# Polysketch attention and a mixture of experts on one core: attention in fewer, wider units at fixed half steps, and fewer changes of TensorE's tile

## The chip, the core and the metric

The kernel runs on 1 core of one Trainium2 chip. The metric is device microseconds (us) of one execution. The kernel is one launch; everything below is inside it.

## What is computed

The reference, cut to what matters (B = 4 batches, H = 4 heads, S = 1088 tokens, head width 32; 4352 tokens of width 128; E = 4 experts with 1024 hidden columns):

```python
def phi(x):
    a = np.einsum('rd,bhsd->bhsr', S1, x)      # r = 8
    b = np.einsum('rd,bhsd->bhsr', S2, x)
    return np.einsum('bhsi,bhsj->bhsij', a, b).reshape(*x.shape[:-1], r * r)
q_p, k_p = (phi(q), phi(k))
kv = np.einsum('bhsf,bhsd->bhfd', k_p, v)
z = np.sum(k_p, axis=2)
attn = np.einsum('bhsf,bhfd->bhsd', q_p, kv) / (np.einsum('bhsf,bhf->bhs', q_p, z)[..., None] + 1e-06)
...
x = attn.transpose(0, 2, 1, 3).reshape(B * S, H * D)
p = domain_probs / (domain_probs.sum(-1, keepdims=True) + 1e-09)
for e in range(E):
    h = np.maximum(x @ w1[e], 0.0)
    out += p[:, e:e + 1] * (h @ w2[e])
```

## The kernel before, in words

**Experts.** Token columns are worked in chunks (`CHUNKS`): 128, 448, 512, seven of 448, and 128 columns, eleven in all. A chunk has 16 steps (4 experts by 4 pairs of 128-wide blocks of hidden columns), a step two half steps, one for each block. The counter `now` numbers the half steps through the whole kernel: chunk m begins at 32m. In chunks 1 to 9 a block's first layer is three fp32r matmuls over 128x128 tiles: xa by wa (L1174), xb by wb (L1175), then ACT scales the partial sum in place in PSUM (L1176, in `first`), and the third, xd by wd (L1226, in `third`), is added behind it. ACT takes relu into ha (L1230), DVE makes hb (L1202) and for two blocks at once hd (L1205, in `lower`). The second layer's passes over ha, hb and hd, or one plain fp32 pass for some blocks, are L1295 in `passed`; `DEAL` sets how many half steps behind its block each pass is issued, `due` holds them and `behind` issues them. Experts 0 and 1 of chunk 1 have a plain fp32 second layer (L1276). POOL weights a result by its gate (L1334, L1336). The gates are loaded by SP (L385), which waits until POOL has left the tile. `turn_back` turns and stores a chunk's output.

**First and last chunk.** With 128 columns they are plain fp32. Their matmuls go through `both` and `on_side` (L257 to L267): a product is done as pairs of matmuls on half tiles, 128 rows by 64 columns of TensorE, the two halves by turns. In the profile all half-tile matmuls have the line L261 and the tile 128*64; an fp32 matmul on half tiles leaves two records.

**Keys.** For each batch `key_pieces` has the pieces: turns of the keys on DVE (L412), projections with full tiles (L456), sums, products on DVE, then `key_sums` (36 half-tile matmuls of 66 columns, `vx` by `kp`) and `key_blocks` (the tile kvx).

**Queries.** The tokens of a batch are cut into units (`UNITS`): [128, 448, 512], [448, 448, 192], [256, 448, 384], [512, 320, 256]. The first two units of batch 0 are worked at the start; the ten others are `later`. A later unit passes through these parts: `unit_turn` (DVE, L596); `unit_project` (four half-tile matmuls with sx, an ACT copy to qs at L787, SP's writes of it to the DRAM tile qd at L789 and its loads back from there, each row repeated, into qp at L796 and qb at L798 or L801); `unit_product`, twice (DVE, L810); `unit_visit` (half-tile matmuls of 66 columns, kvx by qp); `attend_inverse` (DVE, L699 and L704); `attend_scale` (L712); and `unit_out` (turn on DVE at L725, SP's writes to the DRAM tile xd at L744, and loads from there into `ring` or x_last at L753). A chunk's columns are read out of `ring` by ACT (xa, L925) and DVE (xb and xd, L928) in `token_parts`, four steps before the chunk begins. Together on PE come, as one piece named "visit": the key sums of the next batch where the unit is a batch's last, the projection of the next unit, and the products of this one.

**What sets the order.** The instructions of each engine stand in program order. `lay_plan` makes a list of pieces, each with a cost in us and, for some, a piece that it must follow by a number of half steps (`LAND` is 6 for a product behind its visit). In each half step `work` adds to a credit by `rate` and `room` (L1371 to L1386 and L1461 to L1484) and issues pieces from the list's head while the credit lasts; `until_there` issues what is missing when a chunk is near. `holds` counts PSUM banks that attention holds; while there are any, the credit is at least 0.01. PSUM has 6 banks in the pool `ps_h` (first layer and attention) and 2 in `ps_o`. SP issues nearly all DMAs, in program order: the writes and loads above, gates and outputs.

Of the kernel before, what the change touches and what calls it, by code (L numbers as in the profile page):

```python
# [24 lines left out]
def kernel(  # L25
# [26 lines left out]
    P = 128  # L52
# [10 lines left out]
    QW = 512  # L63
    CW = 512
    GE = 160
    LA = 2
    LAND, EARLY = 6, 14
# [15 lines left out]
    UNITS = [[P, 448, 512], [448, 448, 192], [256, 448, 384], [512, 320, 256]]  # L83
# [7 lines left out]
    W2_AT = (36, 38), (41, 43), (45, 47), (65, 67)  # L91
    TOKENS_AT = 11, 12

    CHUNKS = [P, 448, 512] + [448] * 7 + [P]
# [424 lines left out]
    holds = [0]  # L519

    def held(x):
        holds[0] += 1
        return x

    def free(n=1):
        holds[0] = max(0, holds[0] - n)

    def key_pieces(b):

        for r in range(3):  # L530
            add(0.69 if r < 2 else 0.23, lambda r=r: key_turn(b, r), f"turn{r}")
        values, kf = value_copy(b), {}

        def project(gi):
            kf[gi] = held(psum(ps_h, "h"))
            key_project_wide(b, gi, kf[gi])

        def summed(gi):
            key_add(b, gi, kf[gi])
            free()  # L540
            next(values, None)
            if gi == 2 and 1 < b < B - 1:
                load_batch(b + 1)

        for gi in range(3):
            add(0.1, lambda gi=gi: project(gi), f"project{gi}", (f"turn{gi}", 2))
            add(0.2 if gi == 2 else 0.42, lambda gi=gi: summed(gi), f"sum{gi}", (f"project{gi}", 1))
        for p in range(2):
            for x in range(2):
                add(0.76, lambda p=p, x=x: key_product(b, 0, NT, p, x, nc.vector), "products")  # L550
# [3 lines left out]
    def key_sums(b):  # L554
        sums[b] = held(psum(ps_h, "h"))
        for p in range(2):
            key_sum(b, p, sums[b])

    def key_end(b):

        def blocked():
            key_blocks(b, sums.pop(b))
            free()

        if b == 1:
            add(0.1, lambda: key_sums(b), "keysum", ("products", 3))
        add(0.29, blocked, "keyblocks", ("keysum" if b == 1 else "visit", 1))
# [31 lines left out]
    def query_turn(b, c, n):  # L599
        qT = apool.tile([P, QW], F32, tag="qT", name="qT")  # L600
        for _ in query_turns(b, c, n, qT):
            pass
        return qT
# [60 lines left out]
    def attend_products(b, c, n, qp):  # L664

        nd = [held(psum(ps_h, "h")) for _ in range(1 if sum(blocks(m)[0] for _, m in unit_parts(b, c, n)) < 4 else 2)]
# [27 lines left out]
    def attend_inverse(nd, laid):  # L694

        tiles, banks = banks_of(laid)
        rc = apool.tile([P, QW // 32], F32, tag="rc", name="rc")
# [9 lines left out]
    def attend_scale(nd, laid, rc):  # L707

        xs = apool.tile([P, QW], F32, tag="qT", name="xs")
# [8 lines left out]
        free(len(nd))  # L718
        return xs

    def attend_out(b, c, n, laid, xs):

        y = apool.tile([P, QW], F32, tag="y", name="y")
# [35 lines left out]
    qd = dram.tile([B, len(UNITS[0]), HP, QW], F32, name="qd")  # L759
# [63 lines left out]
    def vector_us(n):  # L823

        return 0.16 + n * 1.04e-3

    plan = []

    def add(cost, run, name, after=None):

        plan.append((cost, run, name, after))

    def lay_plan():

        of_first = queries(0, P, UNITS[0][1])
        costs = [0.62] * 9 + [0.05] * 4 + [0.4, 0.55, 0.6, 0.1, 0.1]
        distances = {12: ("first8", 3), 13: ("first12", 1), 16: ("first15", 2), 17: ("first16", 2)}
        for at, cost in enumerate(costs):
            add(cost, lambda: next(of_first, None), f"first{at}", distances.get(at))
        covers.append((len(plan), P + UNITS[0][1]))  # L840
        add(vector_us(later[0][2]), lambda: unit_turn(0), "qturn", ("start", 2 * NQ - 2))
        add(0.1, lambda: unit_project(0), "visit", ("qturn", 6))
        add(0, lambda: None, "wait", ("start", 2 * NQ + 2))
        keys = {}
        for b in range(1, B):
            now_on, plan[:] = list(plan), []
            key_pieces(b)
            keys[b], plan[:] = list(plan), now_on
        for w, (b, c, n, u) in enumerate(later):
            if b == 0:  # L850
                plan.extend(keys[1][:9])
            else:
                at = {(1, 0): (1, 9, 13), (1, 1): (2, 0, 3), (1, 2): (2, 3, 5), (2, 1): (3, 0, 3), (2, 2): (3, 3, 9)}
                if (b, u) in at:
                    k, z0, z1 = at[b, u]
                    plan.extend(keys[k][z0:z1])
                if b == 1 and u == 0:
                    key_end(b)
            more = w + 1 < len(later)
            if more:  # L860
                add(vector_us(later[w + 1][2]), lambda w=w: unit_turn(w + 1), "qturn")
            for p in range(2):
                add(vector_us(n), lambda w=w, p=p: unit_product(w, p), "product", ("visit", LAND if w else LAND + 1))

            last = 0 < b < B - 1 and u == len(UNITS[b]) - 1
            if last:
                plan.extend(keys[b + 1][(5, 9)[b - 1] :])

            def visit(w=w, more=more, then=b + 1 if last else None):
                if then:  # L870
                    key_sums(then)
                if more:
                    unit_project(w + 1)
                unit_visit(w)

            add(0.1, visit, "visit", ("products" if last else "product", 3))
            if last:
                key_end(b + 1)
            add(0.4, lambda w=w: inverse.__setitem__(w, attend_inverse(*products[w])), "inverse", ("visit", 1))
            add(vector_us(n), lambda w=w: over.__setitem__(w, attend_scale(*products[w], inverse.pop(w))), "scale")  # L880
            add(vector_us(n), lambda w=w: unit_out(w), "out")
            covers.append((len(plan), S * b + c + n))

    covers, inverse = [], {}

    def queries(b, c, n):
        qc = early.pop((b, c))
        qf = apool.tile([P, QW], F32, tag="qf", name="qf")
# [3 lines left out]
        free()  # L892
# [120 lines left out]
    def start():  # L1013
# [45 lines left out]
        qT = apool.tile([P, QW], F32, tag="y", name="qT2")  # L1059
# [63 lines left out]
    def first(i, work, between=None):  # L1123
# [3 lines left out]
        if plain(m):  # L1127
# [9 lines left out]
            else:  # L1137
                hp = psum(ps_h, "h")
                for j in range(2):
                    both(  # L1140
                        hp[:, n * j : n * j + n],
                        w1_of[e][:, P * (2 * f + j) : P * (2 * f + j + 1)],
                        (x_last if m else x_first)[:, :],
                        start=True,
                        stop=True,
                    )
# [90 lines left out]
    def second(i, j=None):  # L1237
# [4 lines left out]
        if plain(m):  # L1242
# [3 lines left out]
            for j in range(2):  # L1246
                for _ in range(2):
# [103 lines left out]
    place, now, at_of, credit, spent = [0], [0], {"start": 0}, [0.0], [0.0]  # L1351

    def piece(forced=False):

        if place[0] == len(plan):
            return 0
        cost, run, name, after = plan[place[0]]
        if after and not forced and now[0] < at_of[after[0]] + after[1]:
            return 0
        run()  # L1360
        at_of[name] = now[0]
        place[0] += 1
        spent[0] += cost
        return max(cost, 0.01)

    def until_there(columns):

        while have[0] < columns:
            piece(True)

    def room(hs):  # L1371

        m, kq = divmod(hs // 2, NQ)
        if m == 0:
            return 0.5
        if m == 1:
            return 0.9 if kq < NQ // 2 else 0.2
        if m == 2 and kq < 5:
            return 0.15
        return 0.36 * CHUNKS[m] / CW  # L1380

    rooms = [room(hs) for hs in range(2 * NQ * NC)]
    needed = [0.0] * NC
    for m in range(1, NC):
        upto = next(z for z, columns in covers if columns >= START[m] + CHUNKS[m])
        needed[m] = sum(p[0] for p in plan[:upto])  # L1386
# [41 lines left out]
    def behind(at):  # L1428

        was = closed[0]  # L1430
        while due and due[0][0] <= at:
# [6 lines left out]
            second(i, j)  # L1438
            if f == NP - 1 and j == 1:
                close(m, e)  # L1440
# [17 lines left out]
    for i in range(len(steps) + LA):  # L1458
        if i < len(steps):
            m, kq = steps[i]  # L1460
            until_there(START[m] + CHUNKS[m])  # L1461
            rate = max(
                [0]
                + [
                    (needed[c] - spent[0]) / max(sum(rooms[2 * i : 2 * NQ * c - (EARLY if c > 1 else 13)]), 0.3)
                    for c in range(m + 1, NC)
                    if 2 * NQ * c - (EARLY if c > 1 else 13) > 2 * i
                ]
            )

            def work():

                now[0] += 1
                if not NQ <= i < NQ + 2:
                    credit[0] = min(credit[0] + rate * rooms[min(now[0], len(rooms) - 1)], 0.5)
                if holds[0]:
                    credit[0] = max(credit[0], 0.01)
                while credit[0] > 0:
                    cost = piece()
                    credit[0] -= cost  # L1480
                    if not cost:
                        break
# [67 lines left out]
```

## Time and profile before

| what | value |
| --- | --- |
| median of 3 runs | 448.75 us (448.73 to 449.28) |
| profiled execution | 448.88 us |
| its span, first to last instruction | 447.1 us |
| granted TensorE clock, mean | 1.000 |
| busy: PE, DVE, ACT, POOL | 442.2, 371.4, 333.8, 128.4 us |
| starts of chunks 1 to 10 in the trace | 28.4, 75.0, 125.3, 173.2, 216.9, 263.0, 305.0, 346.2, 386.8 and about 426 us |
| first and last of the ten visits on PE | 50.57 and 349.17 us |

The times of instructions in the profile are within the span; the 1.78 us between the span and the execution's time lie outside it. A line of the timeline has the start, the duration (both in us), the engine, the line of the code, the operation with out<-in, for a matmul the tile of TensorE in use, the shape, and the number of instructions joined in the line; a bracket gives the idle time of the engine before it and what ended it. The end of a matmul is modelled, so its start, and the start of the next, say more than its duration.

### The profile page before, as it was taken

To read this page: it belongs to the slowest core of one execution; us is meant where nothing else is said; L and a number is where in the kernel's file an instruction comes from. 1 tells how busy PE (TensorE), PEld (TensorE's weight loads), DVE (VectorE), ACT (ScalarE), POOL (GpSimd) and SP (SyncE) were. 2 spreads that over 40 slices of the span, in tenths; PEclk is the share of its full clock that TensorE was granted. 3 is DMA by queue.
4 is the path that set the end of the run, shared out by engine and by line. 5 is a ranking of instruction groups with operands and counts; after the bars stand their busy time and mean duration, and the time that the engine had idled before them with its cause. 6 is when DMAs were issued, how large, how long until landed. Compare 5 with 4: busy or idle time off the path is not lost.

```text
span 447.1 us, 8728 instructions
## 1 busy us (share of the span) xinstructions
PE 442.2 (99%) x3030; PEld 370.7 (83%) x3030; DVE 371.4 (83%) x634; ACT 333.8 (75%) x710; POOL 128.4 (29%) x211
## 2 busy tenths in 40 slices
PE   8999999999999999999999999999999999999997
PEld 5887678777788888888888888888888888888887
DVE  5998689897988896888879869898899898898853
ACT  4478878677867876778688767788788888888831
POOL 7346123211323141212321312124223313331430
PEclk9999999999999999999999999999999999999999
DMA  6956264014323402252242142410230021016401
GB/s 194 314 135 173 66 180 95 26 44 115 94 62 86 120 23 81 52 128 71 77 113 28 22 125 66 115 55 21 76 70 22 27 61 40 21 39 216 157 1 30
DMA packets 53620, 38.47 MB, mean 86 GB/s; under 512 B 26920, under 2 KB 49640, under 8 KB 53576
## 3 DMA queue, kind: packets, MB, share of 16 engines
q1 hardware_dynamic: 52776, 37.31, 31.2%
q0 software_dynamic: 576, 0.53, 0.6%
q8 instruction: 24, 0.39, 0.4%
q14 instruction: 20, 0.16, 0.1%
q10 hardware_dynamic: 224, 0.07, 0.1%
HBM read 32.68 MB, written 5.21 MB: 85 GB/s over the span
## 4 chain that ended last, share of the span: by engine, by line
PE 95%; DVE 2%; DMA 1%; issue 0%; SPq 0%; ACT 0%; DVEq 0%; ACTq 0%
PE o L1295 40%; PE h L1226 14%; PE h L1174 13%; PE h L1175 13%; PE h L261 7%; PE o L1276 3%; PE o L261 3%; PE h L456 1%; DMA kn<-in_k_dram 1%; DVE qp L609 1%; DMA vn<-in_v_dram 0%; DVE qa L900 0%; DVE rd L641 0%; DVE kp L478 0%; DVE qf L889 0%
## 5 line engine op out<-in xcount | busy, mean ns | idle before, releaser
L1176 ACT ACTIVATE h<-h 128x448 f32<-128x448 f32 (+1 forms) x288 | 155.5, 540 | 74.9 <-PE h L1175 69.2
L1202 DVE SCALAR_TENSOR_TENSOR hb<-h,ha 128x448 fp32r<-128x448 f32 (+1 forms) x213 | 130.3, 622 | 40.4 <-ACT ha L1230 37.7
L1205 DVE SCALAR_TENSOR_TENSOR hd<-ha,hb 128x896 fp32r<-128x896 f32 (+2 forms) x111 | 123.9, 1116 | 10.7 <-PE o L1295 1.9
L1174 PE MATMUL h<-xa,wa 128*128 128x448 f32 (+1 forms) x288 | 131.5, 457 | 0.0
L1230 ACT ACTIVATE ha<-h 128x448 fp32r<-128x448 f32 (+1 forms) x213 | 116.6, 547 | 0.0
L1334 POOL TENSOR_TENSOR ev<-ev,gate 128x256 f32<-128x256 f32 (+1 forms) x54 | 47.6, 881 | 214.5 <-DVE ev L1327 203.6
L1226 PE MATMUL h<-xd,wd 128*128 128x448 f32 (+1 forms) x288 | 107.3, 373 | 0.1
L1175 PE MATMUL h<-xb,wb 128*128 128x448 f32 (+1 forms) x288 | 105.8, 368 | 0.0
L1295 PE MATMUL o<-ha,vab 128*128 128x448 f32 (+1 forms) x204 | 76.4, 374 | 0.0
L1174 PEld LDWEIGHTS h<-xa,wa 128*128 128x128 f32 x288 | 54.2, 188 | 18.4 <-issue 13.5
L1175 PEld LDWEIGHTS h<-xb,wb 128*128 128x128 f32 x288 | 54.2, 188 | 17.8 <-issue 13.7
L1226 PEld LDWEIGHTS h<-xd,wd 128*128 128x128 f32 x288 | 54.0, 188 | 9.2 <-ACT h L1176 2.3
L1295 PE MATMUL o<-hd,vd 128*128 128x448 f32 (+1 forms) x204 | 60.1, 369 | 0.0
L1295 PE MATMUL o<-hid,w_sb 128*128 128x448 f32 (+1 forms) x118 | 54.7, 545 | 0.0
L1295 PE MATMUL o<-hb,vb 128*128 128x448 f32 (+1 forms) x136 | 50.1, 368 | 0.0
L1336 POOL TENSOR_TENSOR total<-total,ev 128x256 f32<-128x256 f32 (+1 forms) x54 | 45.0, 832 | 4.2
L1235 ACT ACTIVATE hid<-h 128x448 f32<-128x448 f32 (+1 forms) x75 | 41.5, 553 | 0.9 <-PE h L1226 0.8
L1295 PEld LDWEIGHTS o<-ha,vab 128*128 128x128 f32 x204 | 38.3, 188 | 4.2 <-issue 0.2
L1295 PEld LDWEIGHTS o<-hd,vd 128*128 128x128 f32 x204 | 38.1, 188 | 3.6
L1334 POOL TENSOR_TENSOR total<-ev,gate 128x256 f32<-128x256 f32 (+1 forms) x18 | 12.2, 699 | 71.7 <-issue 54.1
L1295 PEld LDWEIGHTS o<-hb,vb 128*128 128x128 f32 x136 | 25.5, 188 | 2.1
L1295 PE MATMUL o<-hb,vab 128*128 128x448 f32 (+1 forms) x68 | 25.3, 372 | 0.0
(151 smaller groups left out, 455.1 us busy)
## 6 DMA issues: line engine op xcount, KB each, us to landing
gate<-gates SPq DMA_DIRECT2D x22, 224.0 KB
kn<-in_k_dram SPq DMA_DIRECT2D x4, 544.0 KB
vn<-in_v_dram SPq DMA_DIRECT2D x16, 128.0 KB
w_last<-in_moe_w_dram SPq DMA_DIRECT2D x4, 512.0 KB
w_sb<-in_moe_w_dram SPq DMA_DIRECT2D x3, 512.0 KB
w_sb<-in_moe_w_dram SPq DMA_DIRECT2D x6, 256.0 KB
qp<-qd SPq DMA_DIRECT2D x6, 224.0 KB
qb<-qd SPq DMA_DIRECT2D x6, 224.0 KB
```

The costliest lines, as they stand in the source:

```text
L261: nc.tensor.matmul(out(s), weights(s), moving(s), **flags)
L1174: nc.tensor.matmul(g, wa[:, e, w], xa, start=True, stop=False)
L1175: nc.tensor.matmul(g, wb[:, e, w], xb, start=False, stop=True)
L1176: nc.scalar.activation(g, g, ACTF.Copy, scale=1.0 + R12)
L1202: nc.vector.scalar_tensor_tensor(out=hb, in0=g, scalar=0.0, in1=high, op0=ALU.max, op1=ALU.subtract)
L1205: nc.vector.scalar_tensor_tensor(out=d2, in0=a2.bitcast(F32), scalar=R12, in1=b2.bitcast(F32), op0=ALU.mult, op1=ALU.subtract)
L1226: nc.tensor.matmul(g, w, x, start=False, stop=True, skip_group_check=True)
L1230: nc.scalar.activation(ha, g, ACTF.Relu, scale=NEAR)
L1235: nc.scalar.activation(hid[i][j], g, ACTF.Relu)
L1295: nc.tensor.matmul(acc[m, e][o][:, 0:n], w, h, start=first_one, stop=last)
L1334: nc.gpsimd.tensor_tensor(out=to[:, x], in0=ev[:, x], in1=g[:, x], op=ALU.mult)
L1336: nc.gpsimd.tensor_tensor(out=total[m][:, x], in0=total[m][:, x], in1=ev[:, x], op=ALU.add)
```

## The change

- The units of batches 1 to 3 become [576, 512]: seven later units and no longer ten. Tiles for queries have QW = 576 columns, those that hold whole blocks of 128 of them XW = 640.
- The chunks become 128, 448, 480, 480, six of 448, and 128; CW, the widest, is 480.
- The plan by costs, credit and `holds` goes. Each piece has a half step of its own, written out in `FIRST_AT`, `KEYS_AT` and `UNITS_AT` (turn, two products, visit). The seven visits are at 47, 79, 111, 143, 175, 207 and 239; the next unit's turn is some half steps ahead of its projection.
- In a visit the products come first, then the next unit's projection, then the key sums where they are due; in the second visit the key sums and blocks of batch 1 and the projection come first, and the products last. Inverse, scaling and turn with its DMAs, which were pieces of their own, are issued in the visit too. The turns of the keys of batches 2 and 3 (three each) are issued at 79 and at 111.
- The first later unit's projection is issued right behind the second layer of chunk 0's last step; the second layer of the step before that uses full tiles, two matmuls in place of four half ones.
- The last chunk's first three steps (`FULL`) use full tiles for the first layer, six matmuls in place of twelve.
- `W2_AT` moves two pieces by a half step each way, and the loops that issued missing pieces become asserts.

In order of PE's instructions the stretches of half-tile matmuls are 17 before and 10 after; PE has 2272 matmuls before and 2248 after, DVE 630 and 611 instructions, ACT 714 and 711, SP 283 and 264 DMAs, POOL 214 and 214. Up to about half step 40 DVE and POOL have the same order.

```diff
-    QW = 512
-    CW = 512
+    QW = 576
+    XW = 640
+    CW = 480
...
-    LAND, EARLY = 6, 14
+    FULL = 3
...
-    UNITS = [[P, 448, 512], [448, 448, 192], [256, 448, 384], [512, 320, 256]]
+    UNITS = [[P, 448, 512], [576, 512], [576, 512], [576, 512]]
...
-    W2_AT = (36, 38), (41, 43), (45, 47), (65, 67)
+    W2_AT = (36, 38), (40, 42), (44, 46), (65, 67)
...
-    CHUNKS = [P, 448, 512] + [448] * 7 + [P]
+    CHUNKS = [P, 448, 480, 480] + [448] * 6 + [P]
...
+    FIRST_AT = (1, 2, 4, 5, 7, 9, 10, 12, 14, 15, 15, 15, 17, 18, 18, 19, 21, 23)
+    KEYS_AT = {
+        1: ((36, 37, 38), (38, 39, 40), (39, 40, 41), (53, 57, 61, 65)),
+        2: ((79, 79, 79), (83, 84, 85), (84, 85, 86), (90, 93, 97, 100)),
+        3: ((111, 111, 111), (115, 116, 117), (116, 117, 118), (122, 127, 148, 153)),
+    }
+
+    UNITS_AT = (
+        (30, 43, 44, 47), (41, 73, 75, 79), (70, 103, 106, 111), (102, 134, 137, 143), (132, 157, 161, 175),
+        (165, 191, 196, 207), (200, 228, 232, 239),
+    )
...
+            def visit(w=w, b=b, c=c, n=n, u=u):
+                more = w + 1 < len(later)
+                if w == 1:
+                    key_sums(1)
+                    key_end(1)
+                    unit_project(w + 1)
+                    unit_visit(w)
+                else:
+                    unit_visit(w)
+                    if more:
+                        unit_project(w + 1)
+                    if 0 < b < B - 1 and u == len(UNITS[b]) - 1:
+                        key_sums(b + 1)
+                rc = attend_inverse(*products[w])
+                over[w] = attend_scale(*products[w], rc)
+                unit_out(w)
+
+            add(at, visit)
...
-                    both(
-                        hp[:, n * j : n * j + n],
-                        w1_of[e][:, P * (2 * f + j) : P * (2 * f + j + 1)],
-                        (x_last if m else x_first)[:, :],
-                        start=True,
-                        stop=True,
-                    )
+                    w = w1_of[e][:, P * (2 * f + j) : P * (2 * f + j + 1)]
+                    if m and kq < FULL:
+                        nc.tensor.matmul(hp[:, n * j : n * j + n], w, x_last[:, :], start=True, stop=True)
+                    else:
+                        both(hp[:, n * j : n * j + n], w, (x_last if m else x_first)[:, :], start=True, stop=True)
...
+                if i == NQ - 2:
+                    o, w = acc[m][:, 0:DM], second_weight(e, 2 * f + j)
+                    nc.tensor.matmul(o, hd[j], w, start=False, stop=False)
+                    continue
...
+            if i == NQ - 1:
+                unit_project(0)
...
             def work():
 
                 now[0] += 1
-                if not NQ <= i < NQ + 2:
-                    credit[0] = min(credit[0] + rate * rooms[min(now[0], len(rooms) - 1)], 0.5)
-                if holds[0]:
-                    credit[0] = max(credit[0], 0.01)
-                while credit[0] > 0:
-                    cost = piece()
-                    credit[0] -= cost
-                    if not cost:
-                        break
+                for run in plan.pop(now[0], ()):
+                    run()
                 for part in at_half.get(now[0] - 1, ()):
                     part()
```

More of the change, by code (lines that the diff above doesn't have):

```diff
@@ L517, in key_blocks, with key_pieces, project_keys, sum_keys @@
         )
[L519 to L528, printed above, removed]
+    def key_pieces(b, turn, project, summed, products):
         for r in range(3):
-            add(0.69 if r < 2 else 0.23, lambda r=r: key_turn(b, r), f"turn{r}")
+            add(turn[r], lambda r=r: key_turn(b, r))
         values, kf = value_copy(b), {}
-        def project(gi):
-            kf[gi] = held(psum(ps_h, "h"))
+        def project_keys(gi):
+            kf[gi] = psum(ps_h, "h")
             key_project_wide(b, gi, kf[gi])
-        def summed(gi):
+        def sum_keys(gi):
             key_add(b, gi, kf[gi])
-            free()
             next(values, None)
@@ L545, in key_pieces @@
         for gi in range(3):
[L546 to L550, printed above, removed]
+            add(project[gi], lambda gi=gi: project_keys(gi))
+            add(summed[gi], lambda gi=gi: sum_keys(gi))
+        for i, (p, x) in enumerate(((0, 0), (0, 1), (1, 0), (1, 1))):
+            add(products[i], lambda p=p, x=x: key_product(b, 0, NT, p, x, nc.vector))
     sums = {}
     def key_sums(b):
-        sums[b] = held(psum(ps_h, "h"))
+        sums[b] = psum(ps_h, "h")
         for p in range(2):
@@ L559, in key_end @@
     def key_end(b):
[L561 to L567, printed above, removed]
+        key_blocks(b, sums.pop(b))
     def unit_parts(b, c, n):
@@ L599, in query_turn @@
     def query_turn(b, c, n):
-        qT = apool.tile([P, QW], F32, tag="qT", name="qT")
+        qT = apool.tile([P, XW], F32, tag="qT", name="qT")
         for _ in query_turns(b, c, n, qT):
@@ L664, in attend_products @@
     def attend_products(b, c, n, qp):
-        nd = [held(psum(ps_h, "h")) for _ in range(1 if sum(blocks(m)[0] for _, m in unit_parts(b, c, n)) < 4 else 2)]
+        nd = [psum(ps_h, "h") for _ in range(1 if sum(blocks(m)[0] for _, m in unit_parts(b, c, n)) < 4 else 2)]
         W = H * (D + 1)
@@ L696, in attend_inverse @@
         tiles, banks = banks_of(laid)
-        rc = apool.tile([P, QW // 32], F32, tag="rc", name="rc")
+        rc = apool.tile([P, XW // 32], F32, tag="rc", name="rc")
         for i, t0, t1 in banks:
@@ L707, in attend_scale @@
     def attend_scale(nd, laid, rc):
-        xs = apool.tile([P, QW], F32, tag="qT", name="xs")
+        xs = apool.tile([P, XW], F32, tag="qT", name="xs")
         banks = banks_of(laid)[1]
@@ L717, in attend_scale @@
             )
-        free(len(nd))
         return xs
     def attend_out(b, c, n, laid, xs):
-        y = apool.tile([P, QW], F32, tag="y", name="y")
+        y = apool.tile([P, XW], F32, tag="y", name="y")
         for c0, T, t0 in laid:
@@ L757 @@
     early = {}
-    qd = dram.tile([B, len(UNITS[0]), HP, QW], F32, name="qd")
+    qd = dram.tile([B, max(len(u) for u in UNITS), HP, QW], F32, name="qd")
     later = [(b, sum(UNITS[b][:u]), n, u) for b in range(B) for u, n in enumerate(UNITS[b]) if b or u == 2]
@@ L821, in unit_out, with add @@
             pass
[L823 to L831, printed above, removed]
+    plan = {}
+    def add(hs, run):
+        plan.setdefault(hs, []).append(run)
+    FIRST_AT = (1, 2, 4, 5, 7, 9, 10, 12, 14, 15, 15, 15, 17, 18, 18, 19, 21, 23)
+    KEYS_AT = {
[3 rows of a table added]
+    }
[3 more added lines that the diff above has]
+    )
@@ L833, in lay_plan @@
     def lay_plan():
         of_first = queries(0, P, UNITS[0][1])
[L836 to L841, printed above, removed]
@@ L842, in lay_plan @@
-        add(0.1, lambda: unit_project(0), "visit", ("qturn", 6))
-        add(0, lambda: None, "wait", ("start", 2 * NQ + 2))
-        keys = {}
-        for b in range(1, B):
[L846 to L882, printed above, removed]
@@ L884 @@
-    covers, inverse = [], {}
+        for at in FIRST_AT:
+            add(at, lambda: next(of_first, None))
+        for w, (b, c, n, u) in enumerate(later):
+            turn, p0, p1, at = UNITS_AT[w]
+            add(turn, lambda w=w: unit_turn(w))
+            for p, hs in enumerate((p0, p1)):
+                add(hs, lambda w=w, p=p: unit_product(w, p))
+            def visit(w=w, b=b, c=c, n=n, u=u):
[15 more added lines that the diff above has]
+            add(at, visit)
@@ L886, in queries @@
+        for b in range(1, B):
+            key_pieces(b, *KEYS_AT[b])
+            if b > 1:
+                add(UNITS_AT[{2: 2, 3: 4}[b]][3], lambda b=b: key_end(b))
     def queries(b, c, n):
         qc = early.pop((b, c))
-        qf = apool.tile([P, QW], F32, tag="qf", name="qf")
+        qf = apool.tile([P, n], F32, tag="qf", name="qf")
         nc.vector.stream_shuffle(in_=qc[:, 0:n], out=qf[:, 0:n], mask=mask_lo)
@@ L891, in queries @@
         nc.vector.tensor_tensor(out=qf[:, 0:n], in0=qc[:, 0:n], in1=qf[:, 0:n], op=ALU.add)
-        free()
         yield
@@ L1058, in start @@
         n1 = UNITS[b][1]
-        qT = apool.tile([P, QW], F32, tag="y", name="qT2")
+        qT = apool.tile([P, XW], F32, tag="y", name="qT2")
         turns = query_turns(b, n, n1, qT)
@@ L1350 @@
     lay_plan()
[L1351 to L1386, printed above, removed]
+    now = [0]
     for i in range(3):
@@ L1460 @@
             m, kq = steps[i]
[L1461 to L1469, printed above, removed]
+            assert have[0] >= START[m] + CHUNKS[m]
             def work():
                 now[0] += 1
-                if not NQ <= i < NQ + 2:
-                    credit[0] = min(credit[0] + rate * rooms[min(now[0], len(rooms) - 1)], 0.5)
-                if holds[0]:
-                    credit[0] = max(credit[0], 0.01)
-                while credit[0] > 0:
-                    cost = piece()
-                    credit[0] -= cost
-                    if not cost:
-                        break
+                for run in plan.pop(now[0], ()):
+                    run()
                 for part in at_half.get(now[0] - 1, ()):
@@ L1488 @@
             if kq == NQ - 4 and 0 < m < NC - 2:
-                until_there(START[m + 1] + CHUNKS[m + 1])
+                assert have[0] >= START[m + 1] + CHUNKS[m + 1]
             for part in to_part.get(i, ()):
@@ L1509 @@
             if m == NC - 2 and kq == NQ // 2:
-                until_there(B * S)
+                assert have[0] == B * S and not plan
                 load_last()
```

## The prediction

> **What bounds the kernel now.** I read the page first, then the waits of PE, the chain, and the timeline around each change of tile.
>
> ```profile
> PE 442.2 (99%) x3030; PEld 370.7 (83%) x3030; DVE 371.4 (83%) x634; ACT 333.8 (75%) x710; POOL 128.4 (29%) x211
> ...
> PEclk9999999999999999999999999999999999999999
> ...
> PE 95%; DVE 2%; DMA 1%; issue 0%; SPq 0%; ACT 0%; DVEq 0%; ACTq 0%
> ```
>
> PE is busy in 99% of the span at the full granted clock, and the chain that ended last is 95% PE. So the time is what PE is given to do: an edit counts if it shortens PE's own list or makes PE wait. The waits of PE are small:
>
> ```profile
> PE h L249 <- PEq L1534: 0.8, 1, 0.8
> PE h L261 <- DVE kT L412: 0.7, 1, 0.7
> PE h L261 <- DVE qp L609: 0.2, 1, 0.2
> PE h L261 <- DVE kvz L501: 0.2, 1, 0.2
> ```
>
> All four lie in the first 28 us, whose instructions stand in the same order in both kernels. A busy PE also hides losses, so I read starts rather than ends: 448-column matmuls start 0.20 us apart (0.23 for 512). Gaps above that, apart from the changes of tile below, add up to 2.2 us (17 of them, 0.07 to 0.35 us). Most are L1226 or the matmul behind it, held by ACT's scaled copy L1176, around 54, 56, 79 and 140 us; one of 0.35 lies at 221.5, and about 0.38 more is inside the half-tile stretch at 126.0.
>
> **Changes of tile.** Attention uses 64-wide half tiles (L261) between full-tile matmuls. PE's timeline around the last visit:
>
> ```profile
> 348.68 0.36 PE L1175 MATMUL h<-xb,wb 128*128 128x448 f32 x1
> ...
> 348.88 0.37 PE L1226 MATMUL h<-xd,wd 128*128 128x448 f32 x1
> ...
> 349.17 0.69 PE L261 MATMUL h<-kvx,qp 128*64 128x66 f32 x16
> ...
> 349.79 0.47 PE L1295 MATMUL o<-ha,vab 128*128 128x448 f32 x1
> ...
> 350.10 0.36 PE L1295 MATMUL o<-hb,vb 128*128 128x448 f32 x1
> ```
>
> The first column is the start. Between full matmuls it steps by 0.20 (348.68 to 348.88). Into the half tiles it steps by 0.29; the 16 records (8 matmuls of two records) take 0.62; the first full matmul keeps PE for 0.31. In the stretch at 83.00, 36 such matmuls take 2.25 us; less the 0.15 found here, 0.058 each. So the 8 should take 0.46, and the change costs (0.29 - 0.20) + (0.62 - 0.46) + (0.31 - 0.20) = 0.36. The 12 half-tile matmuls at 426.77 and those at 29.39 give nearly the same; I take **0.35 us a stretch**.
>
> **The change, part by part.**
>
> 1. Stretches. Before has 17: the start, three around chunk 0's end, ten with visits, the key sums of batch 1 at 83.0, and two at the end (426.8 and 431). After, in the order of PE's instructions, has 10: the start, one behind chunk 0 (second layer and first projection together), seven visits (batch 1's key sums in the second), and one at the end. Seven fewer: 7 x 0.35 = -2.45 us. Where the changes were cheaper than I read, at 0.25, it is -1.75; at 0.40, -2.80.
>
> 2. Matmuls of queries with kvx: 128 become 124, since there are fewer part-filled tiles; 4 x 0.058 = -0.23.
>
> 3. Projections: 40 become 28, over the same columns. Their row goes by columns:
>
> ```profile
> 256.87 1.03 PE L261 MATMUL h<-qT,sx 128*64 128x256 f32 x8
> 257.73 0.69 PE L261 MATMUL h<-kvx,qp 128*64 128x66 f32 x17
> ```
>
> Four matmuls of 256 columns take 257.73 - 256.87 = 0.86, and four of 128 columns at 313.09 took 0.49, 0.05 of it the entry. So 12 fewer with the same columns give 0. The Trainium skill ("TensorEngine Tiling (Array Packing)", Instruction Overhead) has each matmul pay about 60 cycles, so that one column costs what 60 do. Taken as an addition to every matmul, by that the 12 would save an estimated 12 x 60/256 x 0.215 = 0.6 us and the forecast would be 0.6 lower. The trace doesn't agree: 0.44 for 128 columns is half of 0.86 with nothing over.
>
> 4. Full tiles for half tiles: 12 matmuls of x_last become 6, and 4 of chunk 0 become 2. Four L456 of 128 columns (36.23 to 37.12) take 0.22 each, so 6 x 0.22 = 1.33; half ones take (1.46 - 0.15)/12 = 0.11 each, so 12 are 1.31. Together +0.02. Only the stretch goes, counted above.
>
> 5. Chunks: 2 x 480 for 512 + 448 columns. Starts go by columns (0.2025 and 0.2325), so 960 is 960: 0.
>
> 6. DVE, ACT, SP. Fewer units take 19 instructions from DVE, 3 from ACT, 19 DMA issues from SP (qd 6, xd 12, the rest loads, against more ring and gate pieces); POOL has the same 214. None ends the span, so I count 0; the price, where their new places come late, is in the rivals.
>
> Sum of 1 to 6: -2.45 - 0.23 + 0.02 = **-2.66 us**.
>
> 7. Stalls. After the change PE reaches the first visit about 0.38 us earlier, and the products go ahead of the second projection (0.93 us). They need the DVE product L810, which waited for a load:
>
> ```profile
> 50.15 0.69 DVE L810 TENSOR_TENSOR qp<-qp,qb 128x512 f32<-128x512 f32 x1 [1.32 <-DMA qb<-qd]
> ```
>
> It ended at 50.84; PE first used it at 51.8 and would now come at about 50.5. So a new wait of about 0.35 us, between 0 (if the load also comes 0.38 earlier with its projection) and 1.3 (none of it hidden). Queued on PE behind these products are the projection of the next unit and the second layer; all of PE waits. Against that, the 0.38 at 126.0 and the gap of 0.35 at 221.5 sit at steps that are laid out anew, and some of the 54 to 56 us group goes with the spread inverse and scaling. I take 2.2 + 0.38 before, about 2.4 after: **-0.2**, with bounds of +1.5 (as many stalls again, less those that go) and -1.8 (all but the tight L1176 ones gone).
>
> Sum against the profiled execution: it took 448.88 us, 1.78 of it outside the span of 447.1. 448.88 - 2.66 - 0.2 = **446.0 us**. The median of the runs is 448.75, 0.13 lower; the forecast is for the profiled one's level. 0.2% of it is 0.9 us, about what a measurement of this kernel can tell from no change.
>
> **Rivals.**
>
> A. *The bundled DVE work holds PE (slower).* Inverse, scaling and turn come one behind another in the visit's half step, no longer in steps of their own:
>
> ```profile
> L699 DVE TENSOR_SCALAR rc<-h x17: 150/158/171, 21.8 to 353.4; 128x12 f32<-128x12 f32 x8, 128x4 f32<-128x4 f32 x6, 128x8 f32<-128x8 f32 x3
> L704 DVE RECIPROCAL rc<-rc x11: 202/253/254, 22.1 to 353.6; 128x16 f32<-128x16 f32 x6, 128x8 f32<-128x8 f32 x3, 128x12 f32<-128x12 f32 x2
> L712 DVE TENSOR_TENSOR xs<-h,rc x17: 279/424/559, 22.4 to 355.5; 128x384 f32<-128x384 f32 x8, 128x128 f32<-128x128 f32 x6, 128x256 f32<-128x256 f32 x3
> L725 DVE STREAM_TRANSPOSE y<-xs x12: 262/636/712, 23.2 to 366.2; 128x512 f32<-128x512 f32 x6, 128x256 f32<-128x256 f32 x2, 128x384 f32<-128x384 f32 x2, 128x128 f32<-128x128 f32 x2
> ```
>
> Minimum, median and maximum in ns. For 512 columns 2 x 0.16 + 0.25 + 0.56 + 0.28 + 0.71 = 2.1 us, for 576 about 2.4; two visits also take three key turns (two of 0.70, one of 0.23: 1.6). The block can only start when the products are done; beside it PE has the projection (0.9 to 1.0) and 0.2 of leaving the tile. So DVE falls 1.0 to 1.3 us behind, more with key turns. Queued behind are L1202 and L1205, for which PE's L1295 passes wait. From the end of L1202 to its pass the trace of before has a median of 1.9 us and a least of 0.39. The median covers it; the least doesn't, and a half step (1.34 us) at 83% gives DVE back only 0.23. Were a least one due behind each visit, it would cost 7 x (1.15 - 0.39) = 5.3 us, hence 451.3. It decides from 2.86/7 = 0.41 us a visit, and ends beyond no change from 0.54. What speaks against it: the passes behind a visit belong to blocks made two to four half steps earlier. Chance 0.14. On this side stands a rule of the Trainium skill ("Perfetto Trace Analysis", Optimizing Scalar/DVE Operations): if Scalar or Vector aren't saturated but cause bubbles elsewhere, "breaking up instructions may allow work to be completed sooner". The change does the opposite; no run shown here has the work bundled.
>
> B. *Late loads.* Larger units put more bytes between projection, product, xd and ring. In before the loads of a 512-column unit were in 7.1 us after the first issue, of 448 columns 7.0; by that slope 576 need 7.2 to 7.7. The ring came 1.4 to 3 us or more ahead of xa's split on ACT (66.0 against 67.4, 113.5 against 116.6). With out bundled in the visit, the xd writes stand earlier, but behind the next unit's loads. At the first visit that leaves 0 to 0.5 us; were two or three visits late by 0.5 to 1, it costs 1 to 2.5: 447 to 448.5. Chance 0.15, half of it faster by over 0.2%.
>
> C. *The stretches cost less than they seem to* (the matmul behind them gives the time back as a shorter wait for ACT's copy). Then only 1 to 1.5 us go: 447.4 to 447.9. Chance 0.08.
>
> D. *Both gains*: the sum and nearly all removable stalls: 444.3. Chance 0.08.
>
> **How the numbers follow.** The forecast at 446.0 (by its own bounds 445.2 to 447.0) gets 0.55. Faster by over 0.2% (0.9 under the median, 447.85): 0.55 + 0.08 (D) + 0.08 (half of B) + 0.06 (most of C) = 0.77. Within 0.2%: the rest of B and C and the mild part of A, 0.12. Slower: 0.11, the strong part of A. The range goes from D's 444.3 to 448.7, where B ends; it leaves out most of A.
>
> **What would show it.** Right: 10 half-tile stretches in the timeline, each with the steps of 0.29 and 0.31; PE's busy time and the span shorter by some 2.5 to 3 us; the chunks' starts moving ahead by about 0.35 at each visit that is gone, nearly 0.7 of it before 35 us. The first visit with a PE wait of about 0.35 for L810. Rival A would show L1295 waiting for L1202 within two half steps of a visit; B would show PE or ACT waiting behind qb or ring; C would show full matmuls with gaps where the stretches were. The forecast fails if half-tile stretches cost PE much less than 0.35, or if a visit brings more than 0.4 us of waiting.

## The result: no gain, and slightly slower

The changed kernel took 449.55 us (median of 22 runs, 448.42 to 451.15), the kernel before 448.86 beside it (22 runs, 448.56 to 449.28). The ratio is 1.0016, interval 1.0009 to 1.0023: within 0.2% of no change, on the slow side, where 446.0 was forecast. The runs also scatter more: their standard deviation is 0.60 us, 0.20 before. The profiled execution of the changed kernel took 449.22 us with a span of 447.1, the span of before to the tenth.

Not all of the 0.69 is waiting: 0.28 of it lies outside the span. An execution's time less its span is 2.14 us in the 22 runs of the changed kernel (2.10 to 2.19), and 1.86 in those of the kernel before that ran beside the experiments (1.77 to 1.96). The forecast took it as unchanged at 1.78, and no run shows what it depends on. Within the span the changed kernel is slower by about 0.4.

The page of the changed kernel, busy time of each engine and then the shares of the chain that ended last:

```profile
PE 441.1 (99%) x2982; PEld 369.6 (83%) x2982; DVE 372.9 (83%) x615; ACT 334.8 (75%) x707; POOL 129.7 (29%) x211
...
PE 94%; DVE 3%; issue 1%; ACT 1%; DMA 0%; POOL 0%; DVEq 0%; ACTq 0%
```

PE's busy time fell by only 1.1 us, and the chain is no longer as much PE's own: DVE rose from 2 to 3% and ACT from 0 to 1%. The waits of PE say who is meant (us in total, times, longest):

```profile
PE h L250 <- PEq L1459: 0.8, 1, 0.8
PE h L1195 <- ACT h L1145: 0.7, 1, 0.7
PE o L1268 <- DVE ev L1300: 0.4, 1, 0.4
PE o L1268 <- DVE hb L1171: 0.3, 1, 0.3
PE h L262 <- DVE qp L593: 0.2, 1, 0.2
PE h L262 <- DVE kvz L502: 0.2, 1, 0.2
PE h L262 <- POOL sr L315: 0.2, 1, 0.2
```

The second to fourth lines are new; before had no wait of PE after the first 28 us, where the other four lie. The tile ev is an expert's result, which DVE adds up and POOL weights by its gate. (L1195 was L1226, L1145 was L1176, L1171 was L1202, L1268 was L1295, L1300 was L1327.) By starts, the three waits with the slower matmul behind each come to 0.99 near 68 us, and 0.60 and 0.64 near 315 and 322.

**Near 68 us.** ACT's timeline and then PE's:

```profile
66.65 0.54 ACT L1199 ACTIVATE ha<-h 128x448 fp32r<-128x448 f32 x1
68.05 0.60 ACT L896 ACTIVATE xa<-ring 128x480 fp32r<-128x480 f32 x1 [0.86 <-DMA ring<-xd]
68.56 0.53 ACT L1145 ACTIVATE h<-h 128x448 f32<-128x448 f32 x1
```

```profile
68.04 0.37 PE L1144 MATMUL h<-xb,wb 128*128 128x448 f32 x1
69.14 0.47 PE L1195 MATMUL h<-xd,wd 128*128 128x448 f32 x1 [0.73 <-ACT h L1145]
69.45 0.57 PE L1268 MATMUL o<-hd,vd 128*128 128x448 f32 x2
```

PE names ACT's scaled copy L1145, but that is a step of a chain: the copy stood behind xa's split on ACT, and that waited 0.86 us for the ring read. L1195 starts 1.10 behind L1144 where 0.20 is usual. Why the ring was late is seen on SP, in the changed kernel and then in the kernel before:

```profile
57.58 0.60 SPq L781 DMA_DIRECT2D qb<-qd  x1
58.63 1.97 SPq L727 DMA_DIRECT2D xd<-y  x4
65.35 0.82 SPq L736 DMA_DIRECT2D ring<-xd  x2
```

```profile
56.66 0.60 SPq L798 DMA_DIRECT2D qb<-qd  x1
58.73 1.78 SPq L744 DMA_DIRECT2D xd<-y  x4
63.52 0.34 SPq L753 DMA_DIRECT2D ring<-xd  x1
```

The turned unit is ready earlier than before (its turn on DVE starts at 53.19), but its writes to xd are issued at 58.63, behind the next unit's loads, and share the DMA engines with them. These loads are now 576 columns wide and end at 63.63 (448 columns: 61.58). From their first issue (55.53) they took 8.1 us, those of before 7.0 (from 54.62). So xd lands later and the ring read goes out 1.8 us later.

**Near 315 and 322 us.** PE's timeline and then DVE's:

```profile
315.11 0.37 PE L1268 MATMUL o<-ha,vab 128*128 128x448 f32 x1
315.80 0.48 PE L1268 MATMUL o<-hb,vb 128*128 128x448 f32 x1 [0.33 <-DVE hb L1171]
...
322.38 0.37 PE L1268 MATMUL o<-ha,vab 128*128 128x448 f32 x1
323.12 1.02 PE L1268 MATMUL o<-hid,w_sb 128*128 128x448 f32 x2 [0.37 <-DVE ev L1300]
```

```profile
310.92 0.62 DVE L1171 SCALAR_TENSOR_TENSOR hb<-h,ha 128x448 fp32r<-128x448 f32 x1
311.46 0.92 DVE L793 TENSOR_TENSOR qp<-qp,qb 128x512 f32<-128x512 f32 x1
312.30 0.82 DVE L899 SCALAR_TENSOR_TENSOR vm<-w_sb,vm 128x128 fp32r<-128x128 f32 x1
313.05 0.61 DVE L1171 SCALAR_TENSOR_TENSOR hb<-h,ha 128x448 fp32r<-128x448 f32 x1
313.69 1.52 DVE L1174 SCALAR_TENSOR_TENSOR hd<-ha,hb 128x896 fp32r<-128x896 f32 x1
```

This is not behind a visit (the last one is at 324.68) but at the last unit's products, fixed at half steps 228 and 232. There they meet the split of more second-layer weights (vm), and POOL's gating of an expert runs from 311.09 to 314.26: the product takes 0.92, without POOL beside it 0.69; vm 0.82, without it 0.27; hd 1.52, without it 1.09. DVE has no gap over 0.11 from 310.4 to 325 and is late with hb, then with ev.

### The profile page after: what moved, and what is told of

Its sections match the earlier page's. It is cut to its first block, busy times and chain, and to the rows that moved or that the text cites. A ratio compares the mean times of both kernels' runs of the same rounds, so it can differ in the third digit from the quotient of the medians.

```text
span 447.1 us, 8555 instructions
## 1 busy us (share of the span) xinstructions
PE 441.1 (99%) x2982; PEld 369.6 (83%) x2982; DVE 372.9 (83%) x615; ACT 334.8 (75%) x707; POOL 129.7 (29%) x211
## 4 chain that ended last, share of the span: by engine, by line
PE 94%; DVE 3%; issue 1%; ACT 1%; DMA 0%; POOL 0%; DVEq 0%; ACTq 0%
PE o L1268 39%; PE h L1195 13%; PE h L1143 13%; PE h L1144 13%; PE h L262 8%; PE o L1249 3%; PE o L262 3%; PE h L457 1%; DVE hb L1171 0%; DVE qp L593 0%; ACT h L1145 0%; DMA s_raw<-in_S_dram 0%; DVE qa L871 0%; PE h L1113 0%; DVE hd L1174 0%
## 5 line engine op out<-in xcount | busy, mean ns | idle before, releaser
L1145 ACT ACTIVATE h<-h 128x448 f32<-128x448 f32 (+1 forms) x288 | 155.2, 539 | 69.1 <-PE h L1144 62.7
L1171 DVE SCALAR_TENSOR_TENSOR hb<-h,ha 128x448 fp32r<-128x448 f32 (+1 forms) x213 | 131.4, 625 | 38.5 <-ACT ha L1199 35.6
L1307 POOL TENSOR_TENSOR ev<-ev,gate 128x256 f32<-128x256 f32 (+2 forms) x54 | 47.2, 874 | 218.5 <-DVE ev L1300 207.7
L1195 PE MATMUL h<-xd,wd 128*128 128x448 f32 (+1 forms) x288 | 107.1, 372 | 0.8 <-ACT h L1145 0.7
L1144 PE MATMUL h<-xb,wb 128*128 128x448 f32 (+1 forms) x288 | 106.2, 369 | 0.0
L1268 PE MATMUL o<-ha,vab 128*128 128x448 f32 (+1 forms) x204 | 75.7, 371 | 0.0
L1144 PEld LDWEIGHTS h<-xb,wb 128*128 128x128 f32 x288 | 54.2, 188 | 17.8 <-issue 13.6
L1195 PEld LDWEIGHTS h<-xd,wd 128*128 128x128 f32 x288 | 54.0, 187 | 9.2 <-ACT h L1145 2.8
L1268 PE MATMUL o<-hd,vd 128*128 128x448 f32 (+1 forms) x204 | 60.6, 372 | 0.0
L1268 PE MATMUL o<-hid,w_sb 128*128 128x448 f32 (+1 forms) x118 | 55.0, 547 | 0.4 <-DVE ev L1300 0.4
L1268 PE MATMUL o<-hb,vb 128*128 128x448 f32 (+1 forms) x136 | 50.2, 369 | 0.3 <-DVE hb L1171 0.3
L1309 POOL TENSOR_TENSOR total<-total,ev 128x256 f32<-128x256 f32 (+2 forms) x54 | 47.2, 874 | 4.2
L1268 PEld LDWEIGHTS o<-hd,vd 128*128 128x128 f32 x204 | 37.8, 188 | 4.5 <-issue 0.8
L1268 PEld LDWEIGHTS o<-ha,vab 128*128 128x128 f32 x204 | 38.3, 188 | 3.9
L1307 POOL TENSOR_TENSOR total<-ev,gate 128x256 f32<-128x256 f32 (+2 forms) x18 | 11.7, 671 | 66.0 <-issue 43.6
L1268 PEld LDWEIGHTS o<-hb,vb 128*128 128x128 f32 x136 | 25.6, 188 | 3.0 <-DVE hb L1171 0.7
L1268 PE MATMUL o<-hb,vab 128*128 128x448 f32 (+1 forms) x68 | 25.0, 368 | 0.0
```

Source lines behind the costliest of these rows:

```text
L1144: nc.tensor.matmul(g, wb[:, e, w], xb, start=False, stop=True)
L1145: nc.scalar.activation(g, g, ACTF.Copy, scale=1.0 + R12)
L1171: nc.vector.scalar_tensor_tensor(out=hb, in0=g, scalar=0.0, in1=high, op0=ALU.max, op1=ALU.subtract)
L1195: nc.tensor.matmul(g, w, x, start=False, stop=True, skip_group_check=True)
L1268: nc.tensor.matmul(acc[m, e][o][:, 0:n], w, h, start=first_one, stop=last)
L1307: nc.gpsimd.tensor_tensor(out=to[:, x], in0=ev[:, x], in1=g[:, x], op=ALU.mult)
```

## The experiments

All are compared with the kernel before, run beside them on the same chip: 448.82 us beside e1 to e4, 448.99 beside e5 to e8. The ratios go by means. The last column gives the spans, since the time outside them is not the same in all: 2.14 to 2.15 us (means) in the changed kernel and in e1 to e3, 1.78 to 1.87 in e4 to e8 and in the kernel before.

| kernel | runs | median us | against before, ratio (interval) | median span, and of before beside it |
| --- | --- | --- | --- | --- |
| changed kernel | 22 | 449.55 | 1.0016 (1.0009 to 1.0023) | 447.4 |
| e1_ring_first | 11 | 448.90 | 1.0002 (0.9993 to 1.0010) | 446.8, 447.0 |
| e2_products_early | 11 | 448.22 | 0.9988 (0.9979 to 0.9998) | 446.1, 447.0 |
| e3_both | 7 | 447.61 | 0.9972 (0.9961 to 0.9984) | 445.5, 447.0 |
| e4_before_three_fewer | 11 | 447.99 | 0.9982 (0.9973 to 0.9991) | 446.1, 447.0 |
| e5_ring_all | 5 | 447.22 | 0.9966 (0.9954 to 0.9979) | 445.4, 447.1 |
| e6_unbundled | 11 | 449.63 | 1.0012 (1.0004 to 1.0021) | 447.8, 447.1 |
| e7_projections_apart | 11 | 448.86 | 0.9996 (0.9988 to 1.0005) | 447.1, 447.1 |
| e8_slots | 5 | 446.11 | 0.9939 (0.9925 to 0.9952) | 444.3, 447.1 |

**e1_ring_first.** The loads of `unit_project` become a function of their own, `unit_loads`, issued at once everywhere but at the first visit:

```diff
                     unit_visit(w)
                     if more:
                         unit_project(w + 1)
+                        if w:
+                            unit_loads(w + 1)
...
                 unit_out(w)
+                if not w:
+                    unit_loads(w + 1)
```

> The changed kernel, but behind the first visit the loads of unit 1 are issued after unit 0's writes to xd and its ring read, no longer ahead of them. Theory: the seven stretches did give about 2.5 us, and new waits took them back; one is the ring of the first visit, whose writes stood behind the loads of 576 columns (xa waited 0.86 us, PE 0.9 in the profile, and a wait for DMAs would also scatter the times). Then PE's gap near 68 us is gone, the median falls by 0.8 to 1.5 us to 448.1 to 448.7, and the runs scatter no more than those of before (some 0.7 us from lowest to highest). Rival (half-tile stretches cost little, so there was nothing to give back): the wait near 68 goes, but the time stays within 0.3 us of 449.5.

Measured: 448.90, 0.08 over the kernel before where the changed kernel was 0.69 over. On SP the writes and the ring read now stand ahead:

```profile
54.49 2.00 SPq L727 DMA_DIRECT2D xd<-y  x4
58.01 1.12 SPq L736 DMA_DIRECT2D ring<-xd  x2
59.26 0.59 SPq L783 DMA_DIRECT2D qp<-qd  x1
```

The ring is read 7.3 us earlier and the gap near 68 is gone. But the gain is only 0.6, under the 0.8 to 1.5 expected, and the scatter stays (448.15 to 450.13). Two other waits came up in this execution: 0.49 at 50.6 (L797, the product that was L810, behind a load) and 0.47 at 93.5 (DVE late with ev). So a late ring was one part, and the scatter had more than this cause.

**e2_products_early.** One tuple:

```diff
-        (165, 191, 196, 207), (200, 228, 232, 239),
+        (165, 191, 196, 207), (200, 222, 225, 239),
```

> The changed kernel, but the last unit's two DVE products stand at half steps 222 and 225, no longer at 228 and 232. Theory: DVE was late there, since the products (0.92 and 0.69 us) met the splitting of more second-layer weights (vm, L899) and POOL's work; PE waited 0.60 near 315 (hb) and 0.64 near 322 (ev of the expert before). Then both gaps go, 1.0 to 1.25 us, median 448.3 to 448.6, with the scatter of the changed kernel kept. Rival (DVE is late there anyway, by the vm pieces alone): the gaps stay, time within 0.3 us of 449.5.

Measured: 448.22, 0.60 under before, so 1.3 us less than the changed kernel. Both gaps of DVE are gone. In this profile a second ring was late, at the visit of 193 us:

```profile
209.16 0.54 ACT L1199 ACTIVATE ha<-h 128x448 fp32r<-128x448 f32 x1
210.26 0.58 ACT L896 ACTIVATE xa<-ring 128x448 fp32r<-128x448 f32 x1 [0.55 <-DMA ring<-xd]
```

PE lost 0.54 there. This xa reads 256 columns that the visit wrote to the ring. Their packets end at 209.82 here, 0.44 ahead of xa; in the profile of the changed kernel they end at 209.72, and xa starts at 210.10 after an idle time of 0.03. It comes so close that one execution waits and another doesn't.

**e3_both.** Both edits.

> Both edits together. Theory: they add, 449.5 less 1.9 to 2.5, so 447.0 to 447.6, clearly under the kernel before (448.86). Rival (stretches cost little): not under 448.5.

Measured: 447.61, 1.21 under before. Against the changed kernel 0.69 + 1.21 = 1.90, where e1 and e2 gave 0.61 and 1.29: they add.

**e4_before_three_fewer.** The kernel before, with `FULL` and the two full-tile matmuls of chunk 0 from the changed kernel, and

```diff
-        add(0.1, lambda: unit_project(0), "visit", ("qturn", 6))
+        add(0.1, lambda: None, "visit", ("qturn", 6))
...
             second(i, j)
+            if i == NQ - 1:
+                unit_project(0)
```

> The kernel before, with its units and its plan, and only three stretches of half tiles fewer (14 for 17): full tiles for the last chunk's first three steps, full tiles for the second layer of chunk 0's step 14, and the first later unit's projection right behind chunk 0's last second layer. Theory: 3 x 0.35 = 1.05 us less, 447.8, with at most 0.3 of new waiting. Rival (a stretch costs little, below 0.1): 448.6 to 448.9.

Measured: 447.99, 0.83 less, 0.28 a stretch. From the start of chunk 1 to the start of DVE's last instruction the profiles give 1.07 less, 0.35 a stretch. The price holds without new units or fixed half steps: 0.28 by the runs, 0.35 by this one profile.

**e5_ring_all.** As e3_both, with `unit_loads(w + 1)` behind `unit_out(w)` in every visit.

> As e3_both, but in all visits the loads of the next unit are issued behind the writes to xd and the ring read of this one. In the profiles so far the ring's last bytes land 0 to 1 us around xa's start at the visits of 194 and 236 us too (one profile of e2_products_early had PE wait 0.54 near 210). Theory (late rings at several visits are what is left of the loss and its scatter): 0.2 to 0.6 under e3_both, so 447.0 to 447.4, with less than 1 us from lowest to highest. Rival (only the first visit's ring was late): equal to e3_both within 0.2, 447.6.

Measured: 447.22, 1.77 under before, so 0.56 under e3_both by the differences. But this isn't shown to be the rings' worth: the intervals of the two ratios overlap (the means differ by 0.3), and 0.28 of the difference lies outside the span. Within it e5_ring_all is 1.54 under before and e3_both 1.51 (means), so the rival, equal to e3_both within 0.2, isn't ruled out. The last ring packets now end 6 to 11 us ahead of xa at the first five visits (at the one of 194 us: 203.23 against 210.23). What is left of PE's new waits:

```profile
PE h L262 <- DVE qp L797: 0.6, 1, 0.6
PE h L262 <- DVE kT L413: 0.6, 1, 0.6
PE o L1274 <- DVE ev L1306: 0.3, 1, 0.3
```

The middle one is at the start, where before had it too. The first is in the first visit:

```profile
50.27 0.69 PE L262 MATMUL h<-kvx,qp 128*64 128x66 f32 x16
51.61 0.69 PE L262 MATMUL h<-kvx,qp 128*64 128x66 f32 x16 [0.65 <-DVE qp L797]
```

The second half of the visit starts 1.34 behind the first, where 0.51 is its length: 0.82 of waiting. In the profile of the changed kernel this wait is not there. The loads that it hangs on ended at 49.06 in that one, at 49.39 in e3_both, 50.16 here and 49.55 in before, while PE arrives between 49.9 and 50.3: it costs 0 to 0.8 us from one execution to the next. The third line, near 94, comes to 0.55 by starts.

**e6_unbundled.** The changed kernel with the visit's DVE work in half steps of its own:

```diff
-                rc = attend_inverse(*products[w])
-                over[w] = attend_scale(*products[w], rc)
-                unit_out(w)
...
+            add(at + 1, lambda w=w: inverse.__setitem__(w, attend_inverse(*products[w])))
+            add(at + 2, lambda w=w: over.__setitem__(w, attend_scale(*products[w], inverse.pop(w))))
+            add(at + 3, lambda w=w: unit_out(w))
```

> The changed kernel, but a visit's inverse, scaling and turn with its DMAs stand one, two and three half steps behind it, no longer in it. Rival A of the prediction (the bundle makes DVE late for PE): faster than the changed kernel, by 0.4 us a visit that it held, so 447 or less. Theory (the bundle is covered: the trace of the changed kernel shows no gap of PE within two half steps of a visit that the kernel before has not): no gain; as the ring is read some 3 half steps later at the visits where it lands just in time, 449.5 to 452.

Measured: 449.63, 0.64 over before, the changed kernel 0.69: not faster, so Rival A doesn't hold. The equal times hide a difference, though. Outside the span e6_unbundled takes 1.80 us, the changed kernel 2.14; within it e6_unbundled is about 0.4 longer. Its profile shows where: ACT's wait for the ring near 68 is 1.06, 0.20 more, and PE has two new gaps of 0.24 by starts near 205 and 292, where DVE, with inverse, scaling and turn now between its other work, is late with ev. The bundle cost PE nothing that is seen, and taking it apart did.

**e7_projections_apart.** As e5_ring_all, but

```diff
-                    if more:
-                        unit_project(w + 1)
...
+            def apart(w=w):
+                unit_project(w + 1)
+                unit_loads(w + 1)
+
+            add(at, visit)
+            if w != 1 and w + 1 < len(later):
+                add(at + 1, apart)
```

> As e5_ring_all, but in five visits the next unit's projection stands one half step behind the visit, so that PE has 15 stretches of half tiles for 10 and the same matmuls. Theory: 5 x 0.35 = 1.75 us more than e5_ring_all, as the profile reads it. Rival C of the prediction (a stretch costs less than it seems to): less than 5 x 0.15 = 0.75 more.

Measured: 448.86, 1.64 more than e5_ring_all: 0.33 a stretch. By the means, and so by the ratios, it is 1.36 more, 0.27 a stretch; e5_ring_all has only five runs. Both are over the rival's 0.75. One of the five, on PE:

```profile
196.04 0.36 PE L1154 MATMUL h<-xb,wb 128*128 128x448 f32 x1
196.24 0.37 PE L1205 MATMUL h<-xd,wd 128*128 128x448 f32 x1
196.54 1.08 PE L262 MATMUL h<-qT,sx 128*64 128x256 f32 x8
197.55 0.48 PE L1278 MATMUL o<-ha,vab 128*128 128x448 f32 x1
197.87 0.36 PE L1278 MATMUL o<-hb,vb 128*128 128x448 f32 x1
```

The steps are 0.20, then 0.30 into the half tiles, 1.01 for four matmuls that take 0.86 inside a longer stretch, and 0.32 out of them: 0.10 + 0.15 + 0.12.

**e8_slots.** As e5_ring_all, and one tuple:

```diff
-        (30, 43, 44, 47), (41, 73, 75, 79), (70, 103, 106, 111), (102, 134, 137, 143), (132, 157, 161, 175),
+        (30, 43, 45, 48), (41, 73, 78, 79), (70, 103, 106, 111), (102, 134, 137, 143), (132, 157, 161, 175),
```

> As e5_ring_all, but the first visit stands at half step 48 and its second product at 45 (it was 47 and 44), and the second product of unit 1 at 78, not 75. Theory: what is left are two waits of e3_both's profile, 0.38 for L810's operand at the first visit and 0.46 near 93 where DVE was late with ev behind a product; both go: 0.5 to 0.8 under e5_ring_all, 446.4 to 446.8. Rival (they come back elsewhere, DVE being full between 68 and 94 us): within 0.2 of e5_ring_all.

Measured: 446.11 (446.05 to 446.46), 2.88 under before; 0.61% less time, interval 0.48 to 0.75. It is 1.11 under e5_ring_all, more than the 0.5 to 0.8 expected; in the profile of e5_ring_all the two waits were larger, 0.82 and 0.55. PE's waits are those of the first 28 us again, and no others:

```profile
PE h L262 <- DVE kT L413: 0.9, 1, 0.9
PE h L250 <- PEq L1466: 0.8, 1, 0.8
PE h L262 <- DVE qp L593: 0.2, 1, 0.2
PE h L262 <- DVE kvz L502: 0.2, 1, 0.2
```

It has the units, chunks, stretches and bundles of the changed kernel; what differs is the order of the loads on SP and five entries of the plan. It beats both kernels.

## Why the prediction was wrong

**Steps 1 to 4 and the sum of -2.66 held in kind.** The stretches are ten, and each costs about what was read: 0.27 to 0.33 by e7 and 0.28 by e4, for 0.35. Rival C falls with that: the stretches did give about 1.9 to 2.3 us (7 x 0.27 to 0.33), where it had 1 to 1.5. With the waits gone, e8 is 2.88 under before.

**Step 7 is the one that failed.** It took the waiting to change by -0.2 us, at the worst by +1.5, and foresaw one new wait, that for L810. Counted by starts, each step over the usual one for the same matmuls, from 0.05 us up and behind 28.7 us, the trace has 1.4 + 0.1 = 1.5 us of waiting before and 3.4 after, so +1.9, beyond the upper bound. (Two of the prediction's readings are wrong here. The 0.35 at 221.5 isn't a wait: the same gap, 0.35 to 0.37, stands in every kernel wherever a plain fp32 pass is followed by the fp32 projections of the keys. And the 0.38 in the stretch at 126.0 is the own time of four projections, 126.01 to 126.39; the waiting there is two steps of 0.11 and 0.10 for 0.05, the 0.1 of the sum.) The new ones are 0.99 near 68, 0.60 near 315, 0.64 near 322 and some of 0.1 to 0.2, less 0.25 each near 56 and 140 and the 0.1 at 126. They eat 1.9 of the 2.66 in the profiled execution, which itself is 0.33 faster than the median of its runs.

**Outside the span** the forecast carried 1.78 us over from before; the changed kernel's runs have 2.14. That is a term taken as unchanged, and the 0.28 to 0.36 that it rose by is not explained.

**Rival B had the mechanism, at too small a price and chance.** It named the xd writes "behind the next unit's loads" and gave the first visit "0 to 0.5 us"; that visit lost 0.99 and the one of 194 us up to 0.54. It was mis-sized since the landing of the wider loads was taken from the width alone: 7.2 to 7.7 us, where the three loads of 576 columns took 8.1, 9.4 and 8.1 from first issue to last packet. SP holds xd until the loads are issued, and xd's packets then share the engines with the loads': the ring read went out 6.7 us behind xd's first issue, 4.8 in before. e1 shows the worth of it at the first visit, 0.61; what the rings of the other visits cost on the median isn't shown, as e5 can't be told from e3 within the span. (Rival B's own prices end at 448.5; the range that was to end with it was put at 448.7, and the result lies beyond both.)

**DVE's lateness was expected in the wrong place.** Rival A put it behind the visits. There the trace has no new gap, and e6 is not faster than the changed kernel; counted from the second visit's start, the L1171 behind the block does come 1.4 us later than in e6 (103.86 - 95.94 against 102.88 - 96.36), and the slack takes it. The rule of the Trainium skill that was set beside it ("Perfetto Trace Analysis", Optimizing Scalar/DVE Operations: breaking up instructions may allow work to be completed sooner) doesn't apply here, since the work in one piece caused no bubble: e6 spreads it and gains nothing. What cost 1.3 us was a step that the prediction counted as 0: products at fixed half steps 228 and 232, on top of the vm pieces and POOL's work. The plan before chose by credit and had put the last products elsewhere (343.8 us). Step 6 asked only whether DVE had fewer instructions, not what stood beside them in the half steps they were moved to.

**The first visit's wait for L810** was sized at 0.35 between 0 and 1.3: it is 0 in the profiled execution of the changed kernel, 0.38 in e3_both and 0.82 in e5_ring_all. The size lay within what came; that it differs from one execution to the next was not seen. The scatter has at least two sources then, this one and the rings that land around xa's start; how much each gives wasn't separated, but e8, which has neither, stays within 0.4 us over five runs.

**Open.** From the start of chunk 1 to that of DVE's last instruction the changed kernel's profile is 0.36 us shorter than that of before (0.20 more ahead of it, 0.18 more behind it and 0.36 more outside the span make up for that), and e8's 3.15; the sum of -2.66 and the counted gaps (+1.9, and -1.0 in e8) gives 0.8 and 3.7. Some 0.5 is missing in both. A price of 0.28 a stretch, as e4 measured it, would account for it; no run shows that it does.

## What to carry to other kernels

Where an engine is 99% busy, a cheaper list for it buys time only as far as its suppliers keep up: for each step that is moved, look up what else the supplying engine has in that half step, and for each transfer what is issued ahead of it on its queue. Of two transfers, the one that is waited for soonest goes first; here the order of two groups of issues on one queue was worth 0.6 us at the first visit alone and cost nothing. Here the same loads ended over a range of 1.3 us from one execution to another, so a chain that lands within about 1 us of its use isn't on time: it can show as scatter between runs and be missing from the one profile that is read. And compare spans beside times: 0.28 us of this result lay outside the span, and it made e3 and e5 look different and e6 and the changed kernel look equal.

## What the runs showed of the hardware

The granted clock was 1.000 in every profile. A change from 128x128 to 128x64 tiles and back cost 0.27 to 0.33 us by five of them put in (e7), 0.28 by three taken out (e4) and 0.35 by starts, about the time of one and a half 448-column matmuls (0.20 apart), on an engine that the page shows as busy throughout. DVE and POOL were slower where they met: at 311 us a product of 512 columns took 0.92 where 0.69 is usual, and in e2_products_early, where POOL runs at 303.83, the moved product takes 1.08 and POOL's sum of 192 columns 1.41 for 0.60. It depends on the operands: after 34 us in the changed kernel's trace the 55 hd products of 896 columns without POOL beside them took 1.09 each and the 23 with it 1.09 to 1.53, while hb products of 448 columns, which take one operand from PSUM, took 0.58 to 0.63 with and without it. The Trainium skill ("Perfetto Trace Analysis", Optimizing Scalar/DVE Operations) says that GpSimd and DVE share a read port of SBUF; the traces agree in both engines' times, and in that products with both operands in SBUF are the ones slowed. The same loads, first issued between 37.40 and 37.93 us, ended between 48.86 and 50.16 us in the profiles of these kernels, 11.3 to 12.4 us behind their first issue.
